# Chunk-selecting attention and a gated MLP: K and q of the late heads reach their full-height tiles without DMA, and every weight load gets a trigger of its own

## The chip, the cores and the metric

The kernel runs on one core of a Trainium2 chip. The metric is the time on the device in microseconds; the reported value is the median of several executions. Five queues matter. TensorE (PE in the profile) multiplies matrices and writes only to PSUM. VectorE (DVE) and ScalarE (ACT) read PSUM and write SBUF. GpSimd (POOL) works from SBUF to SBUF. SyncE (SP) computes nothing and issues DMA transfers. Each queue runs its instructions in order, so an instruction that waits holds back everything behind it. The engines meet at semaphores.

## The reference

Inputs are q, k, v of shape (4 batches, 8 heads, 768 positions, 64). Positions form 24 chunks of 32. For each query the six best chunks are chosen by a bound, and only these take part in a causal softmax. A gated MLP follows for each batch.

```python
# attention, per batch and head; chunk = 32, top_k = 6, scale = 1/8
k_min, k_max = k_chunks.min(axis=3), k_chunks.max(axis=3)
ub = sum_d maximum(q * k_min, q * k_max)              # bound of each chunk
top_chunks = argsort(where(causal, ub, -1e9))[..., -6:]
mask = chunk_selected & (query position >= key position)
attn = softmax(where(mask, scale * q @ k.T, -1e9))
x = attn @ v                                           # heads side by side: (4, 768, 512)

# MLP, per batch
h = gelu_tanh(x @ w_in)                                # 1024 wide
u, vv = h[..., :512], h[..., 512:]
v_n = (vv - mean(vv)) / sqrt(var(vv) + 1e-6) * g_ln
v_s = w_sg @ v_n + b_sg[:, None]                       # w_sg mixes the 768 positions
out = x + (u * v_s) @ w_out
```

## The kernel before, in words

**Units.** The 32 heads form 16 pairs; one pair's 2 x 64 values of head dimension fill 128 partitions. Pair p belongs to batch p // 4. Two pairs make a quad, for which the chunks are chosen together.

**Loads.** `loads` (L587) issues from SyncE two transfers of 192 KB for each of k, q and v of a pair, one per head. They go into three rotating buffers each (kn, qn, vn). At most four such loads are in flight (WINDOW, L18): a load waits for the one four places before it, and also for its buffer to be free.

**From a load to a score.** `kside` (L599) transposes K on TensorE in two halves of 384 positions (L606, fp32 into a PSG buffer of PSUM). From PSUM, VectorE takes minimum and maximum of each chunk (L612) and ScalarE copies all 128 rows to the bf16 tile KA (L615). `qside` (L628) does the same for q (L635); ScalarE writes the fp32 tile qT (L640), VectorE makes its positive part rT (L644), and GpSimd casts qT to bf16, QA (L646). `vside` casts v (L654). `select` (L660) makes the bounds on TensorE (L672, called UB in the prediction), then on VectorE transposes them, finds the sixth best of each row (L688), marks what is not selected (L691) and transposes the marks into the tile Dt (L695).

**Two forms of scores.** The first six pairs (p < SIDE = 6) are done by `scores` (L709): both heads at once, each in half of TensorE's rows, with a second product that adds a large negative number to what is not selected (L727: IND by Dt). The other ten are done one head at a time by `scores_one` (L751). There a head has a tile of its own of up to 128 rows. The first head uses KA and QA with rows 0 to 63 for the data and rows 64 to 87 for IND and the rows of Dt. The second head uses KB and QB with the data in rows 64 to 127 and the selection in rows 0 to 23. So one product (L770) does both. To fill those tiles, SyncE copies rows 64 to 127 of KA to KB (L623), then IND into rows 64 to 87 of KA (L625), rows 64 to 127 of QA to QB (L649), and four pieces of Dt for each quad (L703). The piece for QA has to wait for the copy QB<-QA, because it overwrites rows that this copy reads; in the same way L625 waits for KB<-KA to land. KB's and QB's own lower rows are set once at the start (L535, L536).

**After the scores.** Scores come in chunks of up to 1024 columns in one of two PSC buffers of PSUM. ScalarE takes the exp into E (L739, L774), GpSimd clears what lies above the diagonal (L746, L778), and TensorE multiplies by v (`head`, L797). VectorE divides by the sum of the row (L805, L807) into XS. `xtrans` turns XS into xT, on TensorE for the first batch, by DMA for most of the others (L815).

**The MLP.** `moe_h` (L847) makes the second half of h (L856, GELU on ScalarE L860, statistics on VectorE) and the first half (L895, L900). `moe_g` makes the product with w_sg (L916, VectorE L929 and L933) and with w_out (L943, L949), and SyncE writes the result (L953). w_sg is transposed once on TensorE (L839), each of its six pieces needing all six loads.

**Weights.** GpSimd issues the loads of w_in (four, winb), w_sg (six, wsgf) and w_out (four, woutb); SyncE issues b_sg and g_ln. `WHEN` (L363) lists for pairs 0 to 3 which of these wait for the first exp of the pair, the "tick".

**What sets the order.** The kernel is not written in the order in which it runs. Every call of `P.op` records an operation with an estimated cost, its inputs and outputs and a priority from the table `URGENCY` (L364). `Program.schedule` (L107) then plays the program through with these costs and appends, for each queue, the operation that can start earliest, the priority deciding among those that start at about the same time. The order that comes out is fixed at build time. `fill` (L238) puts warm-up products (L511) into TensorE's gaps ahead of the first score chunk that uses the second PSC buffer. `link` (L252) finds the semaphore waits.

Of the kernel before, what the change touches and what calls it, by code (L numbers as in the profile page):

```python
# [50 lines left out]
class Program:  # L51
# [55 lines left out]
    def schedule(self):  # L107
        ops = self.ops
# [42 lines left out]
        dma_free = 0.0  # L151
        flight = []
        held = {"pool": 0.0, "dve": 0.0}
        while n < len(ops):
# [59 lines left out]
            if o.dma is not None:  # L214
                dma_free = max(dma_free, t + (1.0 if e == "pool" else 0.2)) + cost
                free[e] = t + (0.9 if e == "pool" else 0.5)
                o.end = dma_free + (2.2 if e == "pool" else 1.6)
            else:
                free[e] = t + cost
                o.end = t + cost  # L220
# [15 lines left out]
        self.seq = sorted(range(len(ops)), key=lambda i: (ops[i].start, ops[i].pos))  # L236

# [14 lines left out]
    def link(self):  # L252
# [5 lines left out]
        for i in self.order["pool"]:  # L258
            if last is not None and last.dma is None and (last.lane or ops[i].lane):
                ops[i].deps[last.idx] = True  # L260
            last = ops[i]
# [51 lines left out]
    def emit(self, nc, ctx):  # L313
# [49 lines left out]
WHEN = [(0, 1), (2, 3, 4, 5), (6, 7, 8, 9, 14), (10, 11, 12, 13)]  # L363
URGENCY = {  # L364
    "load": [-1270, -226, 4288, 330, 7134, 3853, 7531, -486, 8650, 4622, -7, 405, -408, 7239, 12389, 10625],
    "k": [-627, -1578, 6409, 1226, -1011, -989, -877, 5499, 1060, -721, 10255, 11537, 5370, -889, 9494,
        12790],
    "q": [9046, 11456, -1732, 1028, 1052, -1288, -624, -151, -1353, 5984, -777, 4625, -1719, 2066, -1325,
        9604],
    "loadv": [-49, 6178, 6552, -545, 1157, 9509, 8338, 12358, -1570, -337, -183, 5643, 12781, 11157, 4937,  # L370
        6266],
    "v": [10105, 832, 92, -215, 9913, 966, -1182, -68, 2506, -29, 9806, -648, 952, -113, -453, 5188],
    "sel": [-755, 7449, 5823, 11171, -613, 11294, 8514, 11121, 91, 5, 7610, -1146, 9294, 8245, 8926, 12046],
    "sc": [7355, 8473, 9936, 10010, 7502, 465, 11024, 6579, 13059, -9, 300, -1016, 1248, 1593, 7406, -1730],
    "pv": [-102, 5545, -1414, 4832, -208, 6211, -84, 10438, 1365, 99, 774, -315, 119, 9105, -1572, 9599],
    "xt": [-1282, 170, 53, 12001, 8, -824, -770, -1631, -1329, 13392, 8165, 279, 5000, -1395, -816, 1186],
    "wsg": [-722],
    "hv": [474, -2219, -741, 693],
    "hu": [8638, -260, 176, 5783],
    "pt": [223, -589, 246, 9381, -1176, 12120, 1158, 386],  # L380
    "out": [7323, 168, 8486, 4951, -1142, 10653, 6199, 9855],
# [7 lines left out]
def act(n):  # L389
    return 0.12 + n / 1200.0  # L390
# [10 lines left out]
def _kernel(nc, q, k, v, w_in, g_ln, w_sg, b_sg, w_out, out):  # L401
# [45 lines left out]
    with contextlib.ExitStack() as ctx:  # L447
# [96 lines left out]
        def weights(p):  # L544
            after = [("tick", p)]
            for i in WHEN[p]:
# [52 lines left out]
        def kside(p):  # L599
            s, w = p % NQS, p % 4  # L600
            for hf in range(2):
# [9 lines left out]
                for m, op in ((0, ALU.min), (1, ALU.max)):  # L611
# [3 lines left out]
                P.op("act", lambda e, t=t, hf=hf: e.activation(KA[w][:, TG * hf:TG * hf + TG], t.ap()[:, 0:TG],  # L615
                                                               ACTF.Copy),
                     act(TG), reads=[t], writes=[("KA", w, hf), ("KAI", w)], ps=[t])
# [3 lines left out]
            if p < SIDE:  # L621
                return
            P.op("sp", lambda e: e.dma_start(KB[w][64:128, :], KA[w][64:128, :]), 0.4,  # L623
                 reads=[("KAI", w)], writes=[("KB", w)], dma=f"kb{w}")
            P.op("sp", lambda e: e.dma_start(KA[w][64:64 + NC, :], IND[0][0:NC, :]), 0.2,  # L625
                 reads=["IND0", ("KB", w)], writes=[("KAI", w)], dma=f"ki{w}")

        def qside(p):  # L628
            s, w = p % NQS, p % 4
            for hf in range(2):  # L630
                t = ps_g.tile(t_slots(p))

                def tr(e, t=t, hf=hf):
# [12 lines left out]
            P.op("pool", lambda g: g.tensor_copy(QA[w][:], qT[w][:]), gps(S), reads=qk,  # L646
                 writes=[("QA", w), ("QAD", w)])
            if p >= SIDE:
                P.op("sp", lambda e: e.dma_start(QB[w][64:128, :], QA[w][64:128, :]), 0.4,  # L649
                     reads=[("QAD", w)], writes=[("QB", w)], dma=f"qb{w}")  # L650
# [9 lines left out]
        def select(pairs):  # L660
# [36 lines left out]
            for j in range(4):  # L697
                p = pairs[j % len(pairs)]
                w = p % 4
                if p < SIDE:  # L700
                    continue
                qt_, lo, key = (QA[w], 64, ("QAD", w)) if j < 2 else (QB[w], 0, QB[w].name + "D")
                P.op("sp", lambda e, j=j, qt_=qt_, lo=lo: e.dma_start(qt_[lo:lo + NC, :],  # L703
                                                                      Dt[u][32 * j:32 * j + NC, :]), 0.2,
                     reads=[("Dt", u), ("Dt0", u)] + ([("QB", w)] if j < 2 else []), writes=[key],
                     dma=f"D{w}_{j // 2}")


        def scores(p):  # L709
            w, u, ind, es = p % 4, sel_of(p), IND[p % 2], p % 2  # L710
            off = 0
            for c, pieces in enumerate(PIECES):
                t = ps_score.tile()

                def sc(e, t=t, pieces=pieces):
# [26 lines left out]
                    writes=[("E", es, c)] + ([("tick", p)] if c == 0 else []), ps=[t], table="exp")  # L742
# [8 lines left out]
        def scores_one(p, i):  # L751
# [3 lines left out]
                [("KB", w), KB[w].name + "I", ("QB", w), QB[w].name + "D"]  # L755
# [91 lines left out]
        def moe_h(b):  # L847
# [3 lines left out]
            for qt in range(NT):  # L851
                t = ps_g.tile((2, 3))
# [108 lines left out]
        for g in range(NQUAD + 1):  # L961
# [19 lines left out]
            if g >= 1:  # L981
                for p in (2 * g - 2, 2 * g - 1):
# [3 lines left out]
                    for i in range(2):  # L986
                        if p >= SIDE:
                            at("sc", p)
                            P.base += 10 * i
                            scores_one(p, i)  # L990
                        at("pv", p)
                        P.base += 10 * i
                        head(2 * p + i)
                    if p < len(WHEN):
                        P.base = 0.0
                        weights(p)
# [58 lines left out]
```

## Time and profile before

| what | value |
|---|---|
| median of three executions | 244.85 us (243.89 to 246.59) |
| profiled execution, its own time | 244.21 us |
| span in the profile, first to last instruction | 242.5 us |
| mean granted clock of TensorE | 0.977 |
| warm-up products, L511 | 36 recorded, 11.2 us |
| exps on ScalarE, L739 and L774 | 36 and 60, 31.9 and 52.6 us |
| copies of K, L615 | 32, 15.8 us |
| casts of q, L646 | 16, 13.5 us |
| DMA in hardware queues | 30.81 MB, 58.6% of sixteen engines' span |
| DMA issued by GpSimd | 2.75 MB, 7.1% |

The profile shows one execution. Busy time counts an instruction from start to end. TensorE's instructions overlap, so the time that a group really takes is read from the start of one group to the start of the next. The tables of groups give the mean duration of one instruction and the idle time of the engine ahead of it, with what ended it. The 1.7 us between span and time lie outside the instructions.

### The profile page before, as it was taken

To read this page: it belongs to the slowest core of one execution; us is meant where nothing else is said; L and a number is where in the kernel's file an instruction comes from. 1 tells how busy PE (TensorE), PEld (TensorE's weight loads), DVE (VectorE), ACT (ScalarE), POOL (GpSimd) and SP (SyncE) were. 2 spreads that over 40 slices of the span, in tenths; PEclk is the share of its full clock that TensorE was granted. 3 is DMA by queue.
4 is the path that set the end of the run, shared out by engine and by line. 5 is a ranking of instruction groups with operands and counts; after the bars stand their busy time and mean duration, and the time that the engine had idled before them with its cause. 6 is when DMAs were issued, how large, how long until landed. Compare 5 with 4: busy or idle time off the path is not lost.

```text
span 242.5 us, 5827 instructions
## 1 busy us (share of the span) xinstructions
PE 219.0 (90%) x2276; PEld 133.4 (55%) x2292; DVE 184.7 (76%) x532; ACT 148.8 (61%) x224; POOL 76.7 (32%) x103
## 2 busy tenths in 40 slices
PE   7896763989889999999698999999999999999992
PEld 3454342846754657757473565768634677544430
DVE  3958463479876987989475998989689876977982
ACT  2333862769797685658499566787957778463000
POOL 8824750655450304433442100744202122020000
PEclk9999998699999999999799999999999999999999
DMA  8999999499948996988699411184310234201224
GB/s 158 219 218 201 207 212 218 107 169 218 208 107 199 216 210 143 202 137 156 163 269 228 134 30 37 41 221 109 92 30 3 70 117 125 33 0 50 82 85 174
DMA packets 92915, 33.93 MB, mean 140 GB/s; under 512 B 85896, under 2 KB 89176, under 8 KB 92888
## 3 DMA queue, kind: packets, MB, share of 16 engines
q1 hardware_dynamic: 90872, 30.81, 58.6%
q0 software_dynamic: 2016, 2.75, 7.1%
q8 instruction: 18, 0.29, 0.5%
q14 instruction: 9, 0.07, 0.1%
HBM read 24.77 MB, written 6.29 MB: 128 GB/s over the span
## 4 chain that ended last, share of the span: by engine, by line
PE 60%; DMA 25%; DVE 8%; SPq 2%; issue 1%; ACT 1%; POOL 1%; DVEq 0%
DMA qn<-in_q_dram 11%; PE PSG L916 10%; PE PSC L770 9%; PE PSG L943 7%; PE PSG L797 7%; PE PSG L895 7%; PE PSG L856 6%; DMA kn<-in_k_dram 6%; DMA vn<-in_v_dram 5%; PE PSG L672 5%; PE PSG L606 2%; PE PSG L635 2%; DVE vsT L929 2%; PE PSC L721 2%; DMA xT<-XS 1%; DVE osb L949 1%
## 5 line engine op out<-in xcount | busy, mean ns | idle before, releaser
L774 ACT ACTIVATE E<-PSC 128x1024 bf16<-128x1024 f32 (+1 forms) x60 | 52.6, 921 | 18.2 <-PE PSC L770 17.8
L612 DVE TENSOR_REDUCE W<-PSG 128x12 f32<-128x384 f32 x64 | 33.0, 547 | 13.1 <-PE PSG L606 12.9
L739 ACT ACTIVATE E<-PSC 128x1024 bf16<-128x1024 f32 (+1 forms) x36 | 31.9, 930 | 7.4 <-PE PSC L727 7.3
L916 PE MATMUL PSG<-wsgT,vhat 128*128 128x384 bf16 x192 | 35.3, 326 | 0.2
L778 POOL TENSOR_SCALAR_AFFINE_SELECT E<-E 128x768 bf16<-128x768 bf16 x20 | 17.6, 880 | 43.1 <-ACT E L774 43.0
L797 PE MATMUL PSG<-vx,E 128*128 128x65 bf16 x672 | 26.6, 197 | 0.3 <-DVE XS L807 0.3
L797 PEld LDWEIGHTS PSG<-vx,E 128*128 128x128 bf16 x672 | 24.4, 100 | 3.3 <-DVE XS L807 0.7
L916 PEld LDWEIGHTS PSG<-wsgT,vhat 128*128 128x128 bf16 x192 | 17.5, 98 | 13.1 <-DVE vsT L929 1.5
L895 PE MATMUL PSG<-xT,winb 128*128 128x384 bf16 x128 | 24.2, 327 | 0.0
L929 DVE SCALAR_TENSOR_TENSOR vsT<-PSG,glnT,bsgbc 128x384 f32<-128x384 f32 x32 | 19.7, 615 | 5.7 <-PE PSG L916 5.3
L615 ACT ACTIVATE KA<-PSG 128x384 bf16<-128x384 f32 x32 | 15.8, 497 | 12.9 <-DVE W L612 12.9
L943 PE MATMUL PSG<-woutb,uT 128*128 128x512 bf16 x87 | 23.0, 388 | 0.7 <-DVE osb L949 0.2
L635 PE MATMUL PSG<-identF,qn 128*128 128x128 f32 x96 | 15.5, 288 | 8.8 <-DMA qn<-in_q_dram 6.1
L640 ACT ACTIVATE qT<-PSG 128x384 f32<-128x384 f32 x32 | 14.7, 494 | 13.1 <-PE PSG L635 13.0
L949 DVE TENSOR_TENSOR osb<-PSG,XS 128x512 f32<-128x512 f32 x24 | 16.4, 686 | 8.0 <-PE PSG L943 7.4
L646 POOL CAST QA<-qT 128x768 bf16<-128x768 f32 x16 | 13.5, 846 | 28.0 <-ACT qT L640 15.7
L654 POOL CAST vx<-vn 128x768 bf16<-128x768 f32 x16 | 13.9, 870 | 26.2 <-DMA vn<-in_v_dram 12.4
L900 ACT ACTIVATE uT<-PSG 128x384 bf16<-128x384 f32 x32 | 15.7, 491 | 10.3 <-PE PSG L895 9.9
L856 PE MATMUL PSG<-winb,xT 128*128 128x512 bf16 x91 | 21.3, 379 | 0.5 <-DMA xT<-XS 0.3
L860 ACT ACTIVATE vgb<-PSG 128x512 f32<-128x512 f32 x24 | 14.1, 597 | 9.7 <-PE PSG L856 9.6
L863 DVE BATCH_NORM_STATS2 stats<-vgb 128x6 f32<-128x512 f32 x24 | 16.3, 686 | 4.8 <-ACT vgb L860 4.7
L933 DVE TENSOR_TENSOR uT<-vsT,uT 128x384 bf16<-128x384 f32 x32 | 18.3, 573 | 0.5
(71 smaller groups left out, 354.8 us busy)
## 6 DMA issues: line engine op xcount, KB each, us to landing
kn<-in_k_dram SPq DMA_DIRECT2D x32, 192.0 KB, 3.6
qn<-in_q_dram SPq DMA_DIRECT2D x32, 192.0 KB, 4.1
vn<-in_v_dram SPq DMA_DIRECT2D x32, 192.0 KB, 3.8
out_dram<-osb SPq DMA_DIRECT2D x24, 256.0 KB, 2.3
winb<-in_moe_w_in_dram POOLq DMA_DIRECT2D x4, 256.0 KB, 5.6
KB<-KA SPq DMA_DIRECT2D x10, 96.0 KB, 3.2
QB<-QA SPq DMA_DIRECT2D x10, 96.0 KB, 3.1
vhat<-in_moe_w_sg_dram POOLq DMA_DIRECT2D x3, 192.0 KB, 6.1
```

The lines of the kernel that those rows point to most:

```text
L612: P.op("dve", lambda d, t=t, m=m, op=op, hf=hf: d.tensor_reduce(W[w][:, m, 12 * hf:12 * hf + 12], t.ap()[:, 0:TG].rearrange("p (c x) -> p ...
L635: r = e.matmul(t.ap()[:, 128 * j:128 * j + 128], qn[s][:, 3 * hf + j].rearrange("p i d -> p (i d)"), identF[:], is_transpose=True)
L739: P.op("act", lambda e, t=t, n=n, ev=ev: e.activation(ev, t.ap()[:, 0:1024].rearrange("p (i x) -> p i x", x=512)[:, :, 0:n], ACTF.Exp, sca ...
L770: r = e.matmul(t.ap()[:, o:o + n], kt_[rows, 128 * kb:128 * kb + 128], qt_[rows, q0:q0 + n], start=True, stop=True, skip_group_check=True)
L774: P.op("act", lambda e, t=t, c0=c0, c1=c1: e.activation(E[es][:, ETOT * i + c0:ETOT * i + c1], t.ap()[:, 0:c1 - c0], ACTF.Exp, scale=SCALE ...
L797: r = e.matmul(t.ap()[:, 65 * qb:65 * qb + 65], E[es][:, o:o + 128], vx[w][:, kb, i, :], start=(n == 0), stop=(kb == qb), skip_group_check ...
L856: r = e.matmul(t.ap()[:, 0:F], xT[s][:, dk, 128 * qt:128 * qt + 128], winb[:, dk, F:DFF], start=(dk == 0), stop=(dk == NDK - 1))
L895: r = e.matmul(t.ap()[:, 0:TG], winb[:, dk, 128 * fb:128 * fb + 128], xT[s][:, dk, TG * tg:TG * tg + TG], start=(dk == 0), stop=(dk == NDK ...
L916: r = e.matmul(t.ap()[:, 0:TG], vhat[s][:, sb, 128 * fb:128 * fb + 128], wsgT[:, sb, TG * tg:TG * tg + TG], start=(sb == 0 and b not in ROWB),
L929: P.op("dve", lambda d, t=t, fb=fb, tg=tg, vs=vs: d.scalar_tensor_tensor(vsT[vs][:], t.ap()[:, 0:TG], glnT[:, fb:fb + 1], bsgbc[:, TG * tg ...
L943: r = e.matmul(t.ap()[:, 0:DM], gT[s][:, fb, 128 * qt:128 * qt + 128], woutb[:, fb, :], start=(fb == 0), stop=(fb == NF - 1))
L949: P.op("dve", lambda d, t=t, qt=qt, os_=os_: d.tensor_tensor(osb[os_][:].rearrange("p (a c) -> p a c", c=128), t.ap()[:, 0:DM].rearrange(" ...
```

## The change

There are four parts.

1. For the ten late pairs, ScalarE copies K of the first head from PSUM to rows 0 to 63 of KA and K of the second head to rows 64 to 127 of KB, two instructions for each half in place of one. GpSimd casts q in two instructions, rows 0 to 63 to QA and rows 64 to 127 to QB. GpSimd also copies IND into rows 64 to 95 of KA, only for pairs 6 to 9, that is once for each of the four buffers. The three kinds of DMA copies that did this are gone; the four pieces of Dt stay on DMA, and those for QA no longer wait for QB.
2. Every weight load gets its own trigger: a certain score chunk of pairs 0 to 3, and for w_out the first four GELUs of the first batch.
3. The scheduler's model of DMA is another one: two queues that share the bandwidth, and other costs of an issue from GpSimd. `link` now orders GpSimd's computing instructions across DMA issues that stand between them; an instruction with a `lane` waits for the computing instruction before it, and so does the one behind it.
4. The table `URGENCY` has other values throughout, and the small offset between the two heads of a pair is gone. Together with part 3 this gives another order on every queue.

```diff
-WHEN = [(0, 1), (2, 3, 4, 5), (6, 7, 8, 9, 14), (10, 11, 12, 13)]
+WHEN = [[(("tick", 0, 2), 0), (("tick", 0, 4), 1)],
+        [(("tick", 1, 1), 2), (("tick", 1, 4), 3)],
+        [(("tick", 2, 0), 4), (("tick", 2, 2), 5), (("tick", 2, 4), 6)],
+        [(("tick", 3, 0), 7), (("tick", 3, 2), 8), (("tick", 3, 4), 9), (("tick", 3, 5), 14)]]
...
         for i in self.order["pool"]:
-            if last is not None and last.dma is None and (last.lane or ops[i].lane):
+            if ops[i].dma is not None:
+                continue
+            if last is not None and (last.lane or ops[i].lane):
                 ops[i].deps[last.idx] = True
...
-                P.op("act", lambda e, t=t, hf=hf: e.activation(KA[w][:, TG * hf:TG * hf + TG], t.ap()[:, 0:TG],
-                                                               ACTF.Copy),
-                     act(TG), reads=[t], writes=[("KA", w, hf), ("KAI", w)], ps=[t])
+                for kt_, rows, key in ([(KA, slice(0, 128), "KA")] if p < SIDE else
+                                       [(KA, slice(0, 64), "KA"), (KB, slice(64, 128), "KB")]):
+                    P.op("act", lambda e, t=t, hf=hf, kt_=kt_, rows=rows: e.activation(
+                        kt_[w][rows, TG * hf:TG * hf + TG], t.ap()[rows, 0:TG], ACTF.Copy),
+                        act(TG), reads=[t], writes=[(key, w, hf)], ps=[t])
...
-            if p < SIDE:
-                return
-            P.op("sp", lambda e: e.dma_start(KB[w][64:128, :], KA[w][64:128, :]), 0.4,
-                 reads=[("KAI", w)], writes=[("KB", w)], dma=f"kb{w}")
-            P.op("sp", lambda e: e.dma_start(KA[w][64:64 + NC, :], IND[0][0:NC, :]), 0.2,
-                 reads=["IND0", ("KB", w)], writes=[("KAI", w)], dma=f"ki{w}")
+            if SIDE <= p < SIDE + 4:
+                P.op("pool", lambda g: g.tensor_copy(KA[w][64:64 + 32, :], IND[0][0:32, :]), gps(S), lane=64,
+                     reads=["IND0", ("KA", w, 0), ("KA", w, 1)], writes=[("KAI", w)])
...
-            P.op("pool", lambda g: g.tensor_copy(QA[w][:], qT[w][:]), gps(S), reads=qk,
-                 writes=[("QA", w), ("QAD", w)])
-            if p >= SIDE:
-                P.op("sp", lambda e: e.dma_start(QB[w][64:128, :], QA[w][64:128, :]), 0.4,
-                     reads=[("QAD", w)], writes=[("QB", w)], dma=f"qb{w}")
+            if p < SIDE:
+                P.op("pool", lambda g: g.tensor_copy(QA[w][:], qT[w][:]), gps(S), reads=qk,
+                     writes=[("QA", w), ("QAD", w)])
+                return
+            P.op("pool", lambda g: g.tensor_copy(QA[w][0:64, :], qT[w][0:64, :]), gps(S), reads=qk, lane=1,
+                 writes=[("QA", w)])
+            P.op("pool", lambda g: g.tensor_copy(QB[w][64:128, :], qT[w][64:128, :]), gps(S), reads=qk, lane=64,
+                 writes=[("QB", w)])
...
-                     reads=[("Dt", u), ("Dt0", u)] + ([("QB", w)] if j < 2 else []), writes=[key],
+                     reads=[("Dt", u), ("Dt0", u)], writes=[key],
...
-                    writes=[("E", es, c)] + ([("tick", p)] if c == 0 else []), ps=[t], table="exp")
+                    writes=[("E", es, c)] + [("tick", p, c)], ps=[t], table="exp")
...
             for qt in range(NT):
+                if b == 0 and 1 <= qt <= 4:
+                    P.base = 0.0
+                    weights([(("vg", qt - 1), 9 + qt)])
+                    at("hv", b)
```

In the changed order TensorE's queue begins, pair by pair, as follows (K, Q: transposes; S: scores; PV: product with v; XT: xtrans; a dot separates halves or chunks): K0 Q0 K1 Q1 K2 UB0 Q2 K3 Q3, then S0 with UB1 and Q4, S1 with K4, PV0 and Q6, S2 with K5, PV1 and XT0, S3 with K6, PV2 and XT1, then XT2 K7.0 PV3a Q5.0 PV3b Q5.1 K7.1 XT3 Q7.0, and the MLP of batch 0: HV0.0 UB2.0 HV0.1 and then the transposes of w_sg between the other four. The queue before had K0 Q0 K1 Q1 UB0 Q3 K3 K2 Q2, S0 with UB1, then S1 with K4, PV0, Q5 and Q4, and began the MLP of batch 0 behind S5.

## The prediction

> **What bounds the kernel now.** I read the page's busy table and slices first, then the chain of waits in order of time, then busy time stage by stage, then TensorE's own timeline around the one place where it stands still.
>
> ```profile
> span 242.5 us, 5827 instructions
> PE 219.0 (90%) x2276; PEld 133.4 (55%) x2292; DVE 184.7 (76%) x532; ACT 148.8 (61%) x224; POOL 76.7 (32%) x103
> ...
> PEclk9999998699999999999799999999999999999999
> ```
>
> TensorE is 90% busy and nothing else is near it. Of its 219.0 us, 11.2 are warm-up products (L511 x36), so about 208 us are work. Where the missing time lies is shown by stage (columns: stretch and its length, then busy PE, PEld, DVE, ACT, POOL; granted clock; DMA share; GB/s):
>
> ```profile
> 20.00:42.40 22.40, 13.23 (x190) 7.75 (x190) 12.45 (x45) 12.86 (x20) 8.62 (x12) 0.95 1.07 208
> 42.40:60.60 18.20, 16.92 (x249) 11.42 (x248) 13.21 (x42) 13.86 (x21) 10.30 (x16) 0.87 0.91 165
> 60.60:72.60 12.00, 10.45 (x178) 7.78 (x180) 9.58 (x22) 9.80 (x14) 6.46 (x8) 1.00 0.71 156
> 72.60:110.00 37.40, 36.77 (x375) 22.89 (x377) 31.64 (x101) 25.37 (x44) 10.56 (x12) 1.00 0.96 180
> 110.00:130.00 20.00, 17.16 (x176) 12.17 (x176) 13.93 (x35) 15.24 (x23) 6.88 (x9) 0.91 0.93 206
> 130.00:210.00 80.00, 79.55 (x876) 50.03 (x882) 66.85 (x197) 58.10 (x82) 19.31 (x21) 1.00 0.35 89
> ```
>
> From 72.6 us on TensorE hardly rests: 0.6, 2.8 and 0.5 us in three stretches. From 20 to 72.6 it rests 12 us and part of that at a lower clock. The chain of waits (start, length, what) and TensorE's timeline say why:
>
> ```profile
> 26.54 7.33 DMA qn<-in_q_dram
> ...
> 33.89 7.61 DMA qn<-in_q_dram
> ...
> 41.54 0.90 PE PSG L635 x3
> ```
> ```profile
> 31.41 0.23 PE L721 MATMUL PSC<-QA,KA 64*128 64x128 bf16 x2
> ...
> 41.54 0.90 PE L635 MATMUL PSG<-identF,qn 128*128 128x128 f32 x3 [4.13 <-DMA qn<-in_q_dram]
> ...
> 45.62 1.34 PE L797 MATMUL PSG<-vx,E 128*128 128x65 bf16 x21
> ...
> 48.31 0.81 PE L797 MATMUL PSG<-vx,E 128*128 128x65 bf16 x21
> ```
>
> TensorE's queue is in order, and Q of pair 4 stands in it ahead of the scores of pair 2, which need nothing of it. That Q is the 17th pair of loads, and winb and wsgf are landing at the same time. So the start is bound by loads, the rest by TensorE's own work. I call the score products of pair 2 S2, the first product block of the MLP of batch 0 HV0 (L856).
>
> **The change, part by part.**
>
> *SyncE and DMA.* Thirty copies go: KB<-KA and QB<-QA, ten each at 96 KB, and KA<-IND, ten at 36 KB; 2.28 MB, at the 208 GB/s of the second stage 11 us of DMA, all after 59 us. SyncE loses thirty issues of 0.5 to 0.8 us, 9.7 us of waiting for KB<-KA at L625 and 5.8 us at L649 for a reader of QB, with loads queued behind. Only two of these could have held TensorE up, and after 72.6 us it had little to wait for: worth 0 to 2 us. The row DMAs (L703) stay, no longer waiting for QB<-QA; the wait for QA<-Dt (1.9 us at 115.8) was for Dt itself, so I leave it in.
>
> *ScalarE.* K of the ten late pairs leaves PSUM in two ACTIVATEs per half instead of one: 20 more. Each keeps 384 columns, so 0.49 us by L615 (0.44 back to back: two took 0.87): 9.8 us, ACT 149 to 159. If half the partitions halved the price it would be 5. It holds a PSG buffer 0.44 us longer each time, behind the two L612 reductions (1.02 us).
>
> *GpSimd.* QA<-qT (0.83 us) becomes two casts. The nearest row with 64 partitions is KB<-IND, 64x768 in 0.81 to 0.95, the same as for 128, so 10 x 0.83 more, and four copies of IND at 0.88: 11.8 us, POOL 77 to 89 of 240. The new casts and their neighbours wait for each other: 0 to 0.3 us for 48 instructions, no row shows it. Behind them stand v's casts and the triangle masks; POOL sat 43 us waiting for exps at L778, so I take nothing, 2 us at the high end. The rule against it: the Trainium skill (GPSIMD Engine Reference, Key points) says that GpSimd shares its SBUF interfaces with VectorE and contends with two-input or two-port DVE instructions. The trace has such cases, though beside POOL's DMA issues: L619 1.55 us where 0.17 is usual (49.6), L691 1.60 where 0.76 is usual (58.6); with casts L933 stays at a median of 0.557, maximum 1.01. By the rule, all 11.8 us would come on top of DVE's 185 us, some 197 of 240; by the row under 1 us. VectorE has room either way: nothing in the sum.
>
> *Weights.* The 15 transfers are the same, but one per score chunk, from the third exp of pair 0 on. Their four winb no longer meet Q4: in the changed order the loads run K0 Q0 K1 Q1 K2 Q2 v2 K3 Q3 K4 K6 Q4 with Q6, v0 v1 K5 Q7 v3 K7 v4 Q5. Now a wait is added: the transposes of w_sg (L839) stand behind HV0's first two products and wait for the sixth wsgf, triggered by the fifth exp of pair 3 (about 49 us, by the walk below); a wsgf landed 5.5 to 8.5 us after its issue, so 55 to 58. TensorE comes there at 53 + two products of HV0 at 0.86 + half of UB2 at 1.05 = 55.8. I take 1.5 us.
>
> *Order.* This is the large part. The changed instruction order has S0, S1, S2 and S3 in a row, with K4 to K7, Q4, Q6 between, and puts UB2, the w_sg transposes and S4, S5 after HV0 begins. Before, all of them came ahead. I walk this stage:
> - Loads. Pairs landed every 1.7 us (Q1, the fourth, at 10.06; Q2, the eleventh, at 21.8). The ninth, Q3, lands at 18.6, Q4 at about 25.4. S0 then waits for VectorE: its chain to Dt takes until 21.5, as before (S0 was at 22.25).
> - ScalarE from 22.1 us to the first GELU: 20 exps at 0.96 and four small ones at 0.34, 20.6; 18 copies at 0.435, 7.8; together 28.4 us. TensorE's work beside it is 24 us (S pair 2.4, P times V 0.65 a head, 0.35 a transpose group), so ScalarE sets the pace. From 54.96 to 61.4 it ran before without a pause, with the same mix of exps and copies; I take 92% of the time in use: 22.1 + 28.4 / 0.92 = 53.
> - Loads for that point: Q5 is the 21st pair: 25.4 + 8 x 1.75 + four winb at 1.3 + about 3 for wsgf = 47.6. The 1.3 is from 21.8 to 41.5: 19.7 us for seven pairs (12.2) and six weights (7.5). TensorE reaches Q5 at about 50. The loads are 2 us ahead of need, not much.
>
> HV0 thus starts at 53 where it started at 72.6. Still owed then and done before by 72.6: UB2 2.1, L839 2.0, S5 2.4, three chunks of S4 1.4, Q and K halves 0.7: 8.6 us. The rest took 242.5 - 72.6 = 169.9. So 53 + 8.6 + 169.9 + 1.5 = 233.0.
>
> *What is late next.* With the start shortened and 9.8 us more of ScalarE, the stretch from S4 to HV1 has 43.4 us of ACT (34 exps 29, 30 copies at 0.435 13.1, a table load 1.3) against 42.5 of TensorE, and S10 to S13 21.8 against 21.2. Two engines so near each other don't overlap fully; at 95% ScalarE needs 45.7 and 22.9, 4.9 us more than TensorE; some 2.4 us of waits between 95 and 129 are in the 169.9 already. Add 2.5: span 235.5.
>
> *Clock.* The Trainium skill (TensorE: Matmul & The Clock Gate, Part 1) says that an idle window of about 3.4 us halves the clock until TensorE has been busy as long, and Part 4 that transposes don't count as busy. The trace agrees on the first: pauses of 1.59 and 1.93 us cost nothing, the 4.13 did (21 products of P times V in 1.34 instead of 0.81). Part 4 speaks against the change, whose opening has 26 warm-up products for 38 among the same transposes. By it the 16 transpose groups ahead of S0 could take 0.36 more each (0.85 cold at 42.7, 0.49 warm), up to 6 us, most of it in waits for loads; by the row (every slice up to 36 us reads 9, though TensorE rested about 7 us in them) nothing. I take nothing.
>
> The profiled execution took 244.21, 1.7 over its span, and the median is 0.64 above that: 235.5 + 2.3 = about 237.8, stated as 237.5.
>
> **The rivals.**
> 1. *Nothing gained (0.15).* ScalarE, not TensorE, carries the stretches from S4 on, and what the front saves is waited for between S4 and HV1. For it: ACT 43.4 against 42.5. For it too: each late K copy holds a PSG buffer longer. Against: between 130 and 210 TensorE was 99% busy with ACT at 73%. At 86% of ScalarE in use the two stretches need 50.5 and 25.3, 12.1 over TensorE: 233.0 + 12.1 - 2.4 + 2.3 = 245.
> 2. *Slower (0.15): SyncE's loads held behind GpSimd.* The load of v10 must wait for the cast of v7, which now stands on POOL's queue behind four woutb issues, each triggered by a GELU of HV0. Behind v10 on SyncE are Q11, Q10, K9, Q9, which TensorE's order needs from about 76 us. If HV0 comes at 61 rather than 53 (wsgf or Q5 late), the cast is at 69, v10 to Q9 land at 71 to 88, TensorE pauses over 3.4 us again and again and drops its clock: 8 for HV0, 4 of pause, 2.5 of clock from 235.5, 250 with the 2.3. It decides when HV0 comes later than about 59.
> 3. *The change at its headline only (inside 1):* the copies were covered, the order is worth nothing: 244.
>
> **How the numbers follow.** The walk gets 0.70 (231 to 241), rivals 0.15 each. A measurement of this kernel tells about 1% from no change. Inside the walk an HV0 at 50 gives 234.5, at 57 gives 241.5. The range runs from 231 to 246: it leaves out the slow rival and the fast end of the walk. Under 242.4 lie 0.67 of the walk and 0.03 of rival 1; between that and 247.3 the rest of these two, 0.15; slower 0.15.
>
> **What would show it.** Right: no stop of TensorE over 3.4 us between 20 and 60, S3 done by 50, HV0 at 51 to 57, first L839 product waiting for wsgf, ACT near 159 us with 40 new ACTIVATEs of about 0.49, POOL near 89, the L774 exps hardly waiting between 75 and 125. Wrong: a stop at Q5 or at v0, a dropped clock before 60 us, or TensorE idle over 8 us between HV0's end and HV1.

## The result, and the profile after

The changed kernel took 234.01 us (median of four executions, 232.25 to 235.53), the kernel before 245.72 us (four, 243.89 to 246.67) beside it. The ratio is 0.953, its 95% interval 0.942 to 0.964: 11.7 us less. The profiled execution took 232.65 us against 244.21, the span 230.5 us against 242.5.

The page of the changed kernel, the lines that answer to those shown of before:

```profile
span 230.5 us, 5838 instructions
...
PE 214.9 (93%) x2267; PEld 129.5 (56%) x2280; DVE 185.3 (80%) x532; ACT 158.1 (69%) x244; POOL 90.9 (39%) x117
...
PEclk9999799999999999999999999999999999999999
```

TensorE's idle time fell from 23.5 us (242.5 less 219.0) to 15.6. ScalarE and GpSimd do more than before, 9.3 and 14.2 us, VectorE the same. Where the time came from is read by stage (the columns are those of the table shown of before):

```profile
20.00:42.40 22.40, 19.37 (x287) 11.28 (x287) 14.94 (x48) 18.65 (x28) 13.76 (x18) 0.92 1.06 211
42.40:60.60 18.20, 16.36 (x225) 10.54 (x224) 13.92 (x33) 14.74 (x25) 10.06 (x16) 1.00 1.14 229
60.60:110.00 49.40, 49.10 (x598) 32.44 (x598) 43.12 (x142) 40.03 (x62) 26.65 (x31) 1.00 0.89 180
110.00:130.00 20.00, 18.37 (x175) 11.17 (x175) 16.12 (x52) 18.11 (x33) 6.51 (x8) 1.00 0.92 167
130.00:210.00 80.00, 79.24 (x812) 48.12 (x816) 67.05 (x183) 59.72 (x86) 21.43 (x22) 1.00 0.17 45
```

Between 20 and 42.4 us TensorE is busy 19.4 us where it had 13.2. From 60.6 on it hardly rests, as before from 72.6 on. TensorE's timeline marks the places that the prediction spoke of:

```profile
22.99 1.03 PE L691 MATMUL PSG<-qT,W 64*32 64x288 f32 x8 [1.12 <-DVE rT L660]
23.77 1.20 PE L691 MATMUL PSG<-rT,W 64*32 64x288 f32 x8
24.91 0.61 PE L740 MATMUL PSC<-QA,KA 64*128 64x512 bf16 x2
...
50.43 0.55 PE L651 MATMUL PSG<-identF,qn 128*128 128x128 f32 x3
...
54.34 0.81 PE L879 MATMUL PSG<-winb,xT 128*128 128x512 bf16 x3 [0.55 <-DVE xT L846]
...
56.19 1.04 PE L879 MATMUL PSG<-winb,xT 128*128 128x512 bf16 x4
57.07 0.33 PE L858 MATMUL PSG<-identB,vhat 128*128 128x128 bf16 x3
```

HV0 (L879, which was L856) begins at 54.34 where it began at 72.6. Q5 (50.43) waits for nothing. The transposes of w_sg (L858, which was L839) follow HV0's products at once. And at S0 TensorE runs at a lower clock: eight bound products in 1.03 us, where 0.69 is usual, with no longer pause ahead of them than 1.12 us. The point on the clock, below, says why.

The budget of the span: HV0 comes 18.3 us earlier; the prediction put the work then still owed at 8.6. If that estimate holds, this makes 9.7 of the 12.0 us, and the other 2.3 came behind HV0, where the rest took 230.5 - 54.3 - 8.6 = 167.6 us against 169.9.

The two new pieces of work, by shape (count, then busy us and mean ns, then idle time before and what ended it). ScalarE's copies of K first, then GpSimd's casts and the four copies of IND:

```profile
L634 ACT ACTIVATE KB<-PSG 64x384 bf16<-64x384 f32 x20 | 9.7, 486 | 0.3
L634 ACT ACTIVATE KA<-PSG 64x384 bf16<-64x384 f32 x20 | 9.5, 475 | 0.0
L634 ACT ACTIVATE KA<-PSG 128x384 bf16<-128x384 f32 x12 | 6.0, 502 | 9.8 <-DVE W L629 9.8
```
```profile
L668 POOL CAST QB<-qT 64x768 bf16<-64x768 f32 x10 | 8.4, 841 | 2.8 <-PE PSC L789 2.1 <-ACT qT L656 0.3
L666 POOL CAST QA<-qT 64x768 bf16<-64x768 f32 x10 | 8.2, 820 | 10.9 <-PE PSC L746 6.5 <-ACT qT L656 3.7 <-PE PSC L789 0.3
...
L641 POOL COPY KA<-IND 32x768 bf16<-32x768 bf16 x4 | 3.3, 820 | 0.3
```

Half the partitions cost nearly as much as all of them: 0.475 to 0.486 us against 0.502 on ScalarE, and on GpSimd 0.82 to 0.84 against 0.846, the mean of the sixteen 128-row casts of q before.

### The profile page after: what moved, and what is told of

Read it like the earlier page. It is cut to its first block, busy times and chain, and to the rows that moved or that the text cites. A ratio compares the mean times of both kernels' runs of the same rounds, so it can differ in the third digit from the quotient of the medians.

```text
span 230.5 us, 5838 instructions
## 1 busy us (share of the span) xinstructions
PE 214.9 (93%) x2267; PEld 129.5 (56%) x2280; DVE 185.3 (80%) x532; ACT 158.1 (69%) x244; POOL 90.9 (39%) x117
## 3 DMA queue, kind: packets, MB, share of 16 engines
HBM read 24.77 MB, written 6.29 MB: 135 GB/s over the span
## 4 chain that ended last, share of the span: by engine, by line
PE 76%; DVE 10%; ACT 9%; DMA 2%; issue 1%
PE PSG L939 13%; PE PSG L918 10%; PE PSG L966 9%; PE PSC L789 9%; PE PSG L879 8%; PE PSG L691 8%; PE PSG L816 7%; ACT E L758 5%; DVE W L629 3%; PE PSG L623 3%; PE PSG L651 3%; PE PSC L740 2%; PE PSC L528 2%; DMA QA<-Dt 2%; PE PSC L746 1%; DVE rT L660 1%
## 5 line engine op out<-in xcount | busy, mean ns | idle before, releaser
L793 ACT ACTIVATE E<-PSC 128x1024 bf16<-128x1024 f32 (+1 forms) x60 | 52.1, 916 | 7.7 <-PE PSC L789 6.9
L939 PE MATMUL PSG<-wsgT,vhat 128*128 128x384 bf16 x192 | 36.1, 326 | 0.2
L758 ACT ACTIVATE E<-PSC 128x1024 bf16<-128x1024 f32 (+1 forms) x36 | 31.3, 927 | 4.1 <-PE PSC L746 3.6
L797 POOL TENSOR_SCALAR_AFFINE_SELECT E<-E 128x768 bf16<-128x768 bf16 x20 | 18.4, 919 | 37.2 <-ACT E L793 37.0
L816 PE MATMUL PSG<-vx,E 128*128 128x65 bf16 x672 | 25.1, 194 | 0.8 <-ACT E L758 0.5
L816 PEld LDWEIGHTS PSG<-vx,E 128*128 128x128 bf16 x672 | 23.2, 98 | 3.1 <-DVE XS L826 0.9
L939 PEld LDWEIGHTS PSG<-wsgT,vhat 128*128 128x128 bf16 x192 | 17.2, 98 | 13.5 <-DVE vsT L952 1.9
L879 PE MATMUL PSG<-winb,xT 128*128 128x512 bf16 x92 | 22.0, 379 | 1.9 <-ACT vgb L883 0.9
L966 PE MATMUL PSG<-woutb,uT 128*128 128x512 bf16 x88 | 22.1, 380 | 0.5
L634 ACT ACTIVATE KA<-PSG 64x384 bf16<-64x384 f32 (+1 forms) x32 | 15.5, 485 | 9.8 <-DVE W L629 9.8
L892 POOL TENSOR_TENSOR rstd<-rstd,neghalf 128x6 f32<-128x6 f32 x4 | 6.4, 1610 | 32.8 <-DVE rstd L890 32.7
L826 DVE TENSOR_TENSOR XS<-PSG,rden 128x384 bf16<-128x384 f32 x32 | 17.4, 549 | 0.5
```

What stands on the lines that cost most here:

```text
L758: P.op("act", lambda e, t=t, n=n, ev=ev: e.activation(ev, t.ap()[:, 0:1024].rearrange("p (i x) -> p i x", x=512)[:, :, 0:n], ACTF.Exp, sca ...
L793: P.op("act", lambda e, t=t, c0=c0, c1=c1: e.activation(E[es][:, ETOT * i + c0:ETOT * i + c1], t.ap()[:, 0:c1 - c0], ACTF.Exp, scale=SCALE ...
L816: r = e.matmul(t.ap()[:, 65 * qb:65 * qb + 65], E[es][:, o:o + 128], vx[w][:, kb, i, :], start=(n == 0), stop=(kb == qb), skip_group_check ...
L879: r = e.matmul(t.ap()[:, 0:F], xT[s][:, dk, 128 * qt:128 * qt + 128], winb[:, dk, F:DFF], start=(dk == 0), stop=(dk == NDK - 1))
L939: r = e.matmul(t.ap()[:, 0:TG], vhat[s][:, sb, 128 * fb:128 * fb + 128], wsgT[:, sb, TG * tg:TG * tg + TG], start=(sb == 0 and b not in ROWB),
L966: r = e.matmul(t.ap()[:, 0:DM], gT[s][:, fb, 128 * qt:128 * qt + 128], woutb[:, fb, :], start=(fb == 0), stop=(fb == NF - 1))
```

## The experiments

The scheduler rebuilds the whole order when a cost or an edge changes, so a part of the change can't be undone by itself in the source as it stands. In every variant below each queue therefore takes its operations from a fixed list, that of the kernel it starts from, and only the edit named moves anything. All compute the whole of the reference. The kernel before ran beside them on the same chip: 244.47 us beside the first four, 246.08 beside E5 to E8, 244.72 beside E9 and E10. Starts, waits and clocks are from one profile each.

### E1: the order of the change, the copies as before

Theory: the order carries the gain. Rival: the thirty DMA copies carried part of it.

```diff
 # order of every queue: that of the changed kernel
-  ACT  KA rows 0-63 <- PSG; KB rows 64-127 <- PSG   (each half of K, late pairs)
-  POOL QA rows 0-63 <- qT;  QB rows 64-127 <- qT;  IND to KA for pairs 6-9
+  ACT  KA <- PSG, 128 rows
+  POOL QA <- qT, 128 rows
+  SP   KB<-KA, KA<-IND, QB<-QA for each late pair; QA<-Dt waits for QB<-QA
```

> The changed kernel with its order of PE, DVE, ACT, POOL and the loads kept as it is, but K and q of the late pairs moved by DMA again: KB<-KA, KA<-IND, QB<-QA, 30 copies, which SyncE issues as soon as their source is there; one ACTIVATE per half of K, one cast of q. If the gain is the order of the front: ACT back to about 149 us, POOL to about 79, and the time stays within 2 us of the changed kernel's 234, so 232 to 236.5. If the gain comes from a SyncE queue and DMA rings freed of the copies: most of the 11.7 us are lost, 240 to 246. If ScalarE limits the stretch from S4 to HV1, as the prediction's 2.5 us say: it can even be 1 to 2.5 us faster than the changed kernel.

Measured: 234.17 us (233.46 to 235.06, four), ratio to before 0.961 (0.954 to 0.968). ScalarE is at 148.9 us, GpSimd at 78.0, and the kernel is as fast as the changed one, whose three medians were 234.01, 233.02 and 233.87. By the spread of these executions a difference of about 1 us could hide. To that limit the thirty copies cost nothing, and what replaced them costs nothing either. In its profile TensorE (timeline) stopped once for long in the front, and once further on for a product of QA and KA:

```profile
50.61 0.52 PE L733 MATMUL PSG<-identF,qn 128*128 128x128 f32 x3 [2.24 <-DMA qn<-in_q_dram]
...
107.06 1.04 PE L868 MATMUL PSC<-QA,KA 88*128 88x128 bf16 x11 [1.09 <-issue]
```

It had no lower clock at S0, came to Q5 sooner, and waited there for the load; the clock then fell to 0.91 over 42.4 to 60.6 us. HV0 began at 54.49, as in the changed kernel. The wait of 1.09 us reads as a cost of the copies: in the changed kernel the same product waits 0.19 us (105.11). SyncE, with the copies in its queue, issues this quad's QA<-Dt at 104.94 us, and at 101.21 in the changed kernel.

### E2: the order of before, only Q of pair 4 moved

This asks how much of the front is the one stop that the prediction showed.

```diff
 # TensorE, order of before (ScalarE's copies, the positive part and the cast move with it)
-  S1 ... PV0 Q5 Q4 ... S2 ... UB2
+  S1 ... PV0 Q5 ... S2 (five chunks) Q4 ... UB2
```

> The kernel before with its order kept, but the two transposes of Q4 (with their copies, rT and the cast) moved on each queue from ahead of S2 to behind S2's fifth chunk, just ahead of UB2. If TensorE stood still at 37 to 41.5 us only because Q4 is ahead of ready work in its queue: no stop over 3 us there, no dropped clock from 42 to 47, S2 done about 5 us earlier, and 4 to 6.5 us gained, 239 to 241.5 against 245.7. If the front is bound by how fast loads arrive whatever the order: the stop comes back at UB2 or at K6, and at most 2 us are gained, 243.5 to 246.

Measured: 242.68 us (241.37 to 244.1, ten), ratio 0.995 (0.990 to 0.999): 1.8 us gained, by the interval 0.2 to 2.4. TensorE's timeline (two stretches of it):

```profile
46.01 0.69 PE L755 MATMUL PSG<-qT,W 64*32 64x288 f32 x8 [2.18 <-DVE rT L727]
```
```profile
112.63 1.22 PE L853 MATMUL PSC<-QA,KA 88*128 88x128 bf16 x14 [2.03 <-DMA QA<-Dt]
```

The 4.13 us stop and the lower clock of the front are gone, and HV0 began at 67.25, 5.4 us sooner than before. But what followed took 2.5 us longer than before (239.6 - 67.25 against 169.9), among it a wait of 1.56 us at 161.36 for a product of QA and KA that the kernel before doesn't show; the rest I did not follow. The profile is of the fastest of the ten executions. The stop for QA<-Dt between 110 and 120 us stays at 2.03 us with the clock at 0.83. So taking away the stop at Q4 alone brings a part of the gain, not the whole: 1.8 of some 11 us.

### E3: more warm-up products ahead of S0

Theory: the lower clock at S0 comes of too little work of TensorE ahead of it, and costs 2 us. Rival: the front's end is set by something else.

```diff
+FILL2 = {Q3, first half: 1, Q3, second half: 2, UB1: 5}   # warm-up products ahead of these
```

> The changed kernel with eight more warm-up products into an idle PSG buffer: one and two ahead of the halves of Q3, five ahead of UB1, where TensorE stood still for 0.3, 0.6 and 1.1 us and where the granted clock then read 0.83 from 20 to 30 us. Nothing else is changed. If the clock dropped because TensorE did too little work that counts (transposes and short pauses): the clock reads 1.00 from 20 to 30 us, UB1's first eight products take 0.69 and not 1.03, HV0 begins 1 to 2 us earlier than 54.3, and the time is 232 to 233.5. If only a pause of more than 3 us drops it, or the drop has another cause: the dip stays and the time is 234. If ScalarE or a load covers it: the dip goes, HV0 and the time stay.

Measured: 233.18 us (231.44 to 234.76, four), ratio 0.956 (0.946 to 0.966), not told apart from the changed kernel. The clock stayed at 1.00 from 20 to 42.4 us. TensorE then waited for Q5, and the clock fell there:

```profile
51.81 0.87 PE L742 MATMUL PSG<-identF,qn 128*128 128x128 f32 x3 [2.18 <-DMA qn<-in_q_dram]
```

HV0 began at 56.06. The second group of bound products behind S0 begins at 24.77 us, 1.9 sooner than in the changed kernel's profile (26.68), and this was waited away at Q5. That the extra products kept the clock up is not shown by this alone: E10, below, has the full clock there without them.

### E4: the order of the change, the weights triggered as before

```diff
-WHEN = [[(("tick", 0, 2), 0), (("tick", 0, 4), 1)],
-        [(("tick", 1, 1), 2), (("tick", 1, 4), 3)],
...
+WHEN = [[(("tick", 0, 0), 0), (("tick", 0, 0), 1)],
+        [(("tick", 1, 0), 2), (("tick", 1, 0), 3), (("tick", 1, 0), 4), (("tick", 1, 0), 5)],
...
```

> The changed kernel with the weights triggered as before: winb 0 and 1 behind the first exp of pair 0, winb 2 and 3 and wsgf 0 and 1 behind that of pair 1, wsgf 2 to 5 behind that of pair 2, woutb behind that of pair 3; in POOL's queue they stand ahead of the mask of that chunk. All else in the changed order. If the order of the front makes the gain: Q4, Q6 and v0 arrive up to 2 to 4 us later behind weights, part of it covered, 235 to 238. If the single triggers make the gain: TensorE stops for more than 3 us between 25 and 50 us and 6 us or more are lost, 240 to 246.

Measured: 238.51 us (236.65 to 238.87, four), ratio 0.977 (0.969 to 0.985). Against the kernel before (244.47), the change with the old triggers is worth some 6 us. The single triggers are worth some 4 more: E1, which has them, took 234.17 on the same chip, 4.3 us less by the medians, 3.9 by the means, with about 1.6 to either side. TensorE's timeline, then GpSimd's:

```profile
29.80 0.90 PE L734 MATMUL PSG<-identF,qn 128*128 128x128 f32 x3 [3.31 <-DMA qn<-in_q_dram]
...
55.84 0.52 PE L734 MATMUL PSG<-identF,qn 128*128 128x128 f32 x3 [2.10 <-issue]
...
59.78 1.21 PE L958 MATMUL PSG<-winb,xT 128*128 128x512 bf16 x4
```
```profile
22.55 1.30 POOL L648 DMA_DIRECT2D winb<-in_moe_w_in_dram  x2 [0.20 <-issue]
...
34.03 1.08 POOL L648 DMA_DIRECT2D winb<-in_moe_w_in_dram  x2 [0.46 <-ACT E L841]
35.10 1.08 POOL L653 DMA_DIRECT2D vhat<-in_moe_w_sg_dram  x2
```

At the first exp of pair 0 two loads of winb go out together, at 22.55 us, beside the two of Q4. The trace has all four landings: winb at 26.33 and 28.66, Q4 at 28.93 and 29.76. In E1 the first winb goes out at 25.83, and Q4 is there at 26.09 and 26.95, so 2.8 us earlier. TensorE waits 3.31 us for Q4; the burst of four weights (34.03 and 35.10) comes only behind this stop. Then it waits 2.10 us for Q5, whose second transfer lands at 55.75, in E1 at 50.52. A lower clock went with each wait (29.4 to 36.3 and 56.8 to 60.2 us), and HV0 came at 59.78, 5.4 us later than in the changed kernel. From 60.6 to 110 us TensorE then did not rest (49.40 of 49.40 us busy).

### E5 to E8: the load of Q5 two places earlier

E1 and E3 both ended at Q5, the last load of the front. E6 puts its two transfers in front of those of Q7, v3, K7 and v4. E5 is the changed kernel unaltered, beside them on the same chip. E7 adds to E6 the warm-up products of E3. E8 adds to E6 the copy of K by one ACTIVATE per half and KB<-KA by DMA for pairs 6 and 7, four ACTIVATEs less at the front's end.

```diff
 # SyncE, order of the changed kernel
-  v1 K5 Q7 v3 K7 v4 Q5
+  v1 K5 Q5 Q7 v3 K7 v4
```

> The changed kernel once more, on the chip of the next three. Either theory: 232 to 235.5. What is asked is where HV0 begins and where the clock drops: if it hangs on the phase of a free-running window, the drop now stands elsewhere than at 22 to 26 us, as it did in the two kernels before, where it stood at 50 to 53; if it belongs to UB1, it is at 22 to 26 again.

> The changed kernel with one thing moved: the two loads of Q5 stand on SyncE behind those of K5, so ahead of Q7, v3, K7 and v4. If TensorE's start is held at its end by the arrival of Q5 (waits of 2.2 us at about 50 us in the two runs that had no early drop of the clock): no wait for qn at 50, HV0 at 52.5 to 53.5 and everything behind it in step, 1 to 3 us gained against the changed kernel on the same chip, 231 to 233. If ScalarE's queue sets HV0, as the prediction's walk had it: HV0 stays at 54 and so does the time. If v3 or K7 now come too late: a wait at PV3 instead.

> The same with the eight extra warm-up products of the earlier run. If the clock, then the loads held the front: no drop of the clock before 60 us, HV0 at 52 to 53, 230.5 to 232.5. If ScalarE's queue holds it: as the kernel without them.

> Q5 early, and K of pairs 6 and 7 in one ACTIVATE per half with KB<-KA on DMA, so four ACTIVATEs of 0.49 us less in ScalarE's queue ahead of HV0. If ScalarE sets HV0 once Q5 is early: HV0 1 to 1.8 us earlier than with Q5 early alone, 230 to 232. If not: no difference; two more copies in a full DMA can cost up to 1 us.

| kernel | median (range, n) | HV0 | longest waits ahead of it, 44 us on |
|---|---|---|---|
| E5, as changed | 233.02 (230.88 to 234.92, 6) | 54.40 | none for Q5; at S0 2.23 for rT, then a lower clock |
| E6, Q5 early | 231.19 (230.90 to 232.13, 5) | 52.32 | 0.96 and 0.78 for XS |
| E7, and warm-ups | 231.74 (230.66 to 233.02, 6) | 53.06 | 1.27 and 0.94 for XS |
| E8, and four ACTIVATEs less | 232.27 (232.01 to 233.27, 5) | 53.24 | 0.65 for xT, 0.82 for XS |

TensorE's timeline of E6 at the front's end:

```profile
46.67 0.51 PE L925 MATMUL PSG<-identB,XS 128*128 128x128 bf16 x6 [0.96 <-DVE XS L909]
49.45 0.82 PE L899 MATMUL PSG<-vx,E 128*128 128x65 bf16 x21 [0.78 <-DVE XS L909]
...
52.32 1.04 PE L962 MATMUL PSG<-winb,xT 128*128 128x512 bf16 x4 [0.32 <-DVE xT L929]
```

The wait for qn is gone and HV0 is 2 us earlier. Neither warm-ups nor fewer copies on ScalarE add to that. E7 is above E6 by less than its spread. E8 is above it by 1.1 us (about 0.7 to either side), as its expectation allowed for two more copies by DMA; which of its two edits does it wasn't followed. What remains there are short waits for VectorE's results.

### E9 and E10: E6 and the changed kernel once more

The ranges of E5 and E6 overlap, so both ran again side by side on another chip.

> The kernel with Q5's two loads directly behind K5's once more, beside the changed kernel on the same chip. If the load of Q5 is what holds the front's end: 1 to 2 us below the changed kernel's median again (the first pair of runs had 231.19 beside 233.02, ranges overlapping), HV0 at 52 to 53 with no wait for qn ahead of it. If the first difference was chance of the clock: within 0.5 us of the changed kernel, with dropped clocks as often.

> The changed kernel unaltered, the other half of the comparison: 232.5 to 234, its executions spread over 3 to 4 us, since in some of them TensorE's clock drops at S0 or at Q5 and in others not; granted clock between 0.988 and 1.0.

Measured: E9 232.06 us (230.95 to 233.76, six), ratio to before 0.953 (0.946 to 0.959); E10 233.87 us (232.66 to 235.76, six), 0.960 (0.952 to 0.968). The means differ by 1.50 us in the first pair (1.09 without E5's slowest execution, 234.92) and by 1.81 in the second; together 1.65 us (1.45), with about 0.9 to either side from the spread of the executions. E6 is the fastest kernel here, 0.7% under the changed one.

The two profiles show two more things. First, TensorE's timeline of E10, the same program as the changed kernel:

```profile
22.77 0.69 PE L691 MATMUL PSG<-qT,W 64*32 64x288 f32 x8 [1.11 <-DVE rT L660]
...
50.62 0.87 PE L651 MATMUL PSG<-identF,qn 128*128 128x128 f32 x3 [2.15 <-DMA qn<-in_q_dram]
```

Here the clock was full at S0 (0.69 us after a pause of 1.11, against 1.03 after 1.12), and the wait for Q5 was 2.15 us with a lower clock behind it. The same kernel loses its time at one place or at the other. Second, in E9, first TensorE's timeline, then GpSimd's:

```profile
53.92 1.04 PE L962 MATMUL PSG<-winb,xT 128*128 128x512 bf16 x4
57.15 0.33 PE L941 MATMUL PSG<-identB,vhat 128*128 128x128 bf16 x3 [2.19 <-issue]
```
```profile
50.47 0.82 POOL L756 CAST vx<-vn 128x768 bf16<-128x768 f32 x1 [2.87 <-DMA vn<-in_v_dram]
51.23 0.53 POOL L653 DMA_DIRECT2D uT<-in_moe_w_sg_dram  x1
```

The sixth piece of w_sg was issued at 51.23 us, because it stands on GpSimd's queue behind a cast of v that waited 2.87 us for its load. By the trace it landed at 57.06, and TensorE went on at 57.15, after 2.19 us. The profile labels that wait "issue"; the landing shows what it was. In the changed kernel the last piece was issued at 49.53 and landed at 54.49, and TensorE came at 57.07.

## Why the prediction was right, point by point

The forecast was 237.5 us, the measured median 234.01, inside the range. The mechanism held: the new order and the single triggers carry the gain, and the copies carry none that these runs can tell. E4 is the change without its triggers, some 6 us; the triggers add some 4. That the 6 are the order's is by exclusion, since E1 takes the copies out. Two of its signs of being wrong came all the same, a lower clock before 60 us in the changed kernel's profile and a stop at Q5 in E10, the same program; each took about 2 us in its profile. Of its signs of being right, the wait for w_sg stayed away.

**SyncE and DMA, 0 to 2 us.** It was 0 to about 1 us: E1 has the copies and is as fast. What the prediction left in, the stop for QA<-Dt with its lower clock (1.89 us at 117.7, granted 0.75 and 0.57 in the 5 us behind it), is gone, but by the order: E2 with the copies and the old order still has it (2.03), E1 with the copies and the new order has the 1.09 us at 107.06 and the full clock there. In the changed kernel this stretch shows only:

```profile
115.81 0.62 PE L789 MATMUL PSC<-QB,KB 128*128 128x128 bf16 x7 [0.49 <-ACT E L793]
116.77 0.81 PE L879 MATMUL PSG<-winb,xT 128*128 128x512 bf16 x3 [0.34 <-DVE XS L826]
120.23 1.90 PE L879 MATMUL PSG<-winb,xT 128*128 128x512 bf16 x8 [0.75 <-ACT vgb L883]
```

**ScalarE, 9.8 us more.** Measured 9.3, with 0.475 to 0.486 us for 64 rows against the 0.49 taken; the other possibility, half the rows at half the price, is excluded.

**GpSimd, 11.8 us more.** Measured 14.2: the casts of q 8.6 more (22.1 against 13.5), the copies of IND 3.3, so 11.9 as worked out; the other 2.3 lie in instructions of the same number that took longer, 1.6 of them in the masks of L765 and L797; why isn't shown. The rule of the Trainium skill weighed there, GpSimd contending with VectorE, would have brought VectorE to some 197 us; it measured 185.3 against 184.7. The row was the right guide, with VectorE at 80%.

**Weights, a wait of 1.5 us.** Not spent in the changed kernel: the last piece landed at 54.5, just ahead of the 55 to 58 that were worked out, and TensorE came at 57.07 and not at 55.8. The wait is real, though. E9, which came to HV0 at 52.07, paid 2.19 us there. The single triggers as such were not priced in the prediction; E4 puts them at some 4 us, about a third of the gain.

**Order.** HV0 at 53, measured 54.34, 54.40 and 55.68 in three profiles. S0 at 21.5, measured 20.89. S3 done by 50, measured 48. "The loads are 2 us ahead of need, not much" is a step that failed: TensorE waited 2.24, 2.18 and 2.15 us for Q5 in E1, E3 and E10, when no lower clock had slowed it before. Q5 landed at 50.5 in E1 and E10 and at 51.7 in E3, and not at 47.6. Some 1.6 us of that were there at Q4 already, which landed at 27.0 in all three and not at 25.4; the rest came in the loads behind it. In the profile of the changed kernel itself this was hidden: Q5 landed at 49.5, and TensorE, after the lower clock at S0, came only at 50.4.

**ScalarE as the next limit, 2.5 us.** Mis-sized, and its sign with it: behind HV0 the kernel took 2.3 us less than 169.9, not 2.5 more. ScalarE did come to its limit, 9.8 us busy of 10 from 110 to 120 us, and TensorE rested 1.6 us from 110 to 130. But the 2.8 us of rest and the lower clock that stood there before had gone. That twenty ACTIVATEs less don't help is E1: with ScalarE 9 us lower TensorE is busy 18.44 of these 20 us against 18.37.

**Clock, nothing taken.** This step failed too: TensorE ran at half clock from 23.2 to 26.6 us in the first profile, where the prediction expected the full clock. The twelve traces show what goes with such a fall. Within each of them the times between changes of the clock are multiples of 3.41 us (the kernel before: 40.23, 47.05, 118.73 and 122.15 us; the changed one: 23.21 and 26.63), so the changes lie on a grid, and the grid lies elsewhere in each profile. What goes with a fall is how long TensorE rested within the one stretch of the grid ahead of it. Four such stretches, each from its own profile (the changed kernel, E10 twice, E9; length, then TensorE's busy time):

```profile
19.80:23.21 3.41, 1.71 (x34) 1.17 (x37) 3.10 (x6) 3.09 (x5) 1.66 (x2) 1.00 0.82 170
18.87:22.28 3.41, 1.98 (x32) 1.32 (x32) 3.38 (x8) 2.37 (x5) 0.95 (x1) 1.00 1.26 218
46.17:49.58 3.41, 1.65 (x30) 1.30 (x30) 2.30 (x6) 2.75 (x6) 2.11 (x3) 1.00 1.20 240
53.37:56.79 3.42, 1.58 (x16) 0.39 (x8) 1.17 (x3) 2.05 (x4) 2.29 (x4) 1.00 0.98 168
```

The clock fell behind the first and the third, and stayed behind the second and the fourth. In the changed kernel the pauses of 0.58 and 1.12 us ahead of the bound products lie in one stretch, 1.70 us of rest; in E10 the border at 22.28 us cuts the second pause in two. All ten falls of the twelve traces, from 6 us to 3 us before the end, follow a stretch with 1.70 to 2.96 us of rest. Of the some 750 other stretches at full clock, the fourth above has 1.83 and none else more than 1.59.

Part 1 of the Trainium skill's page (TensorE: Matmul & The Clock Gate) states that the window is free-running and that one kernel varies from run to run by it; the traces agree. What Part 1 says of the idleness it takes, about 3.4 us, is not what they show: half of that was enough. I had set aside Part 4 of that page, that transposes don't count as busy, and these traces don't speak for it: with transposes counted as rest, a stretch with 2.71 us kept the clock (E7, from 9.8 us) and one with 1.90 lost it (the kernel before, from 115.3), so the two kinds come apart less well.

One fall costs about 2 us here (the second group of bound products behind S0 begins at 26.68 us, and at 24.82 in E10), and the twelve executions of E5 and E10 spread from 230.9 to 235.8 us with mean clocks of 0.982 to 1.0. So whether the front loses its time at S0 or at Q5 in one execution is partly chance of the grid.

**The rivals.** Nothing gained, and the headline only: fell with the result. Slower, by loads held behind v7's cast from an HV0 later than about 59: didn't come about, as HV0 came at 54. (Its sum, 235.5 + 8 + 4 + 2.5 + 2.3, is 252.3 and not 250.) E4 with 59.78 shows no rest of TensorE behind it; but there the woutb issues stand elsewhere, so that chain itself wasn't tried.

The forecast was 3.5 us too high. In the span the terms make -5.0: HV0 +1.3, the wait for w_sg -1.5, and the stretch behind HV0 -4.8 (-2.3 where +2.5 had been put). What lies around the span gives 1.5 back: 2.15 us between the span and the profiled time instead of 1.7, a median 1.36 us above the profiled execution instead of 0.64, and 0.3 from the rounding. That the forecast came this near is in part luck: it left out the lower clock and put the loads too early, and it put the stretch behind HV0 too long by more.

**What stays open.** Part 1 of the change alone in the order of before wasn't tried: there K of pair 10 is transposed ahead of the scores that still read the KB it would be copied to, so that order isn't free of the change. Part 3's new ordering of GpSimd's instructions was not run by itself. What exactly is weighed in a stretch of 3.41 us isn't settled, as 1.83 us of rest kept the clock once and 1.70 and 1.76 lost it.

## What to carry to other kernels

When a kernel's order is rebuilt together with a data path, freeze the order and swap the path alone: here the named change was worth nothing that could be measured, and the order and the spread of fifteen weight loads carried the gain. In a queue that runs in order, a load's due time has to be walked for each consumer in the new order, with a margin larger than the error of the walk; the wait for Q5 and that for w_sg were both within 2 us of need, and each appeared as soon as TensorE came 2 us sooner. Before putting an engine's added work on the path, look for the waits that the new order removes from the same stretch; here ScalarE was busy 98% of 110 to 120 us, and TensorE rested less there than before.

## What the runs showed of the hardware

- The granted clock changes on a grid of 3.41 us that lies elsewhere in each profile. It fell behind stretches of it with 1.70 to 2.96 us of rest of TensorE, whether in one pause or several, and, but for one with 1.83, stayed behind those with 1.59 or less. A pause across a border counts in two stretches: after 2.18 us (E2, up to 46.0, border at 45.1) the clock stayed, after 2.24 us within one stretch (E1, at Q5) it fell.
- Two weight loads of 256 KB that GpSimd issued at 22.55 us (E4) and not from 25.83 on (E1) went with two loads of 192 KB from SyncE landing 2.8 us later.
- Copies of 64 partitions cost nearly what those of 128 do, at the shapes above (0.475 to 0.486 us against 0.502 on ScalarE, 0.82 to 0.84 against 0.846 on GpSimd); a copy of 32 rows on GpSimd took 0.82 us as well.
- With 14 us more work on GpSimd, VectorE's busy time was 0.6 us higher in 185.
